# Gated linear attention on one core: a chunk of 64 tokens in place of 128

## The chip, the cores and the metric

The kernel runs on one core of a Trainium2 chip. The core's engines work side by side, each through its own instruction list in order: TensorE (PE in the profile; PEld is its weight load), VectorE (DVE), ScalarE (ACT), GpSimd (POOL), and SyncE (SP), which issues the DMAs. The metric is device time in microseconds (us).

## The reference, cut to what matters

```python
B, H, S, D = 4, 8, 768, 48
mag = np.sqrt(a_re * a_re + a_im * a_im)
scale = np.minimum(mag, 0.999) / (mag + 1e-06)          # a_n = a * scale
for t in range(S):                                       # per batch and head
    S_re, S_im = ar * S_re - ai * S_im + kv, ar * S_im + ai * S_re   # kv = outer(k_t, v_t)
    y[:, :, t] = einsum('bhd,bhde->bhe', q[:, :, t], S_re)
x = y as (B, S, H * D)                                   # 384 channels
xk, xr = mu * x + (1 - mu) * x_prev                      # two mixes, token t with t - 1
out = sigmoid(xr @ w_r) * (maximum(xk @ w_k, 0) ** 2 @ w_v)      # d_ff = 1024
```

A complex state per head is rotated and decayed at each token, and read by q. The result goes through a channel mix with three weight matrices.

## The kernel before, in words

The work is cut into 8 **units** of U = 384 tokens (4 batches, two halves each; `half` is 0 or 1). A unit has three parts.

- `gate(u)`, on ACT and DVE: cumulative log decay and angle over the tokens, by which k and q are multiplied in place in `G[u]` (`kqc` and `kqs` are its cosine and sine rows, channels on partitions). With that, the recurrence is plain causal linear attention over stacked rows of 2 x 48 per head.
- `attend(u)`. `stack(h)` moves a head's rows by DMA into a tile `kq[h]` with k in `[:, 0]` and q in `[:, 1]`. The tokens form NC = 3 chunks of P = 128. `scores(h)` (tile `sc`, one PSUM bank) multiplies k by q within each chunk, and DVE multiplies by a causal mask into `pt`. `advance(c)` transposes the keys of chunk c (`tr`, three per part, copied by ACT into `kt`), multiplies them by the values (`up`, 96 x 384), and DVE adds this to the running `state`. `values(p)`, for a pair of heads, adds values times `pt` (`f0`) and state times q (`f1`) in one bank `y`; the two heads go to partitions 0 to 63 and 64 to 111, the two column halves of the array. ACT copies `y` to `ys`, DMAs carry it to `X[u]`.
- `mix(u)`: `x` split in a high and a low part, `z` (11 blocks of nine matmuls of 128 x 384), squared relu into `hhi` and `hlo`, `o` (8 blocks of nine), the gate and the store. These matmuls are float32r, one load and one matmul each. The attention's products are float32: each appears in the trace as **two** load-and-matmul pairs, whereas the instruction rows shown further down count products.

Before the first units, weights are converted on ACT, DVE and POOL (`wx`).

`Plan` sets the order: every piece of work is an op with an engine, a cost, data it reads and writes, and slots that it uses (PSUM banks `ps` 5, `kq` 6, `pt` 3, `v` 5, `ys` 1 ...). It computes due times backwards, simulates the engines, and emits instructions in the order that this gives; each engine then runs its list as written and waits where data are missing. `attend(u)` is laid beside `mix(u - 1)`, so PE's list mixes the two, and `gate(u + 2)` is laid under them.

Of the kernel before, what the change touches and what calls it, by code (L numbers as in the profile page):

```python
# [30 lines left out]
YS = 3  # L31
# [23 lines left out]
PTS = 3  # L55
# [184 lines left out]
def tile_kernel(ctx, tc, gat, vt, w_all, mu, slow_g, slow_v, out):  # L240
# [40 lines left out]
    def op_dma(n, f, **kw):  # L281
# [6 lines left out]
    mask = keep.tile([P, P], F32, name="mask")  # L288
    nc.gpsimd.memset(mask, 1.0)
    nc.gpsimd.affine_select(out=mask, in_=mask, pattern=[[1, P]], compare_op=ALU.is_ge,  # L290
                            fill=0.0, base=0, channel_multiplier=-1)
# [13 lines left out]
    state = [keep.tile([2 * D, C], F32, name=f"state{i}") for i in range(NC)]  # L305
# [8 lines left out]
    def open_mix(stack):  # L314
# [5 lines left out]
                wx=WBUFS, g=GP, v=5, sq=1, m=1, ph=1, kq=KQ, kt=2, pt=PTS, xt=1, ys=YS)  # L320
# [8 lines left out]
    def mix(u):  # L329
# [51 lines left out]
        def gate_r(mt):  # L381
# [10 lines left out]
            op_pe(1.45, mul, reads=parts(1) + [("w", W_R + ct) for ct in range(NT)], writes=[("z", u, mt)],  # L392
# [7 lines left out]
        def first(j):  # L400
# [23 lines left out]
            op_pe(1.45, mul, reads=parts(0) + [("w", W_K + 2 * j)], writes=[("f", u, j)], uses=[sp, part_slot[0], sr, sh])  # L424
# [5 lines left out]
        def second(j):  # L430
# [8 lines left out]
            op_pe(1.45, mul, reads=[("hhi", u, j), ("hlo", u, j), ("w", W_V + 2 * j)] + [("o", u, j - 1)] * (j > 0),  # L439
# [22 lines left out]
    with ExitStack() as fast:  # L462
# [71 lines left out]
        def gate(u):  # L534
# [17 lines left out]
            def load_v(c):  # L552
                def f():
                    v = ap.tile([P, C], F32, tag="v", name="v", bufs=5)
# [158 lines left out]
        def attend(u):  # L713
# [6 lines left out]
            def stack(h):  # L720
# [3 lines left out]
                def move(r0, n, i):  # L724
                    def f():
                        if h not in kq:
                            kq[h] = ap.tile([2 * D, 2, U], F32, tag="kq", name="kq", bufs=KQ)
                        ct, o = r0 // P, r0 - h * D
                        s = slice(r0 - ct * P, r0 - ct * P + n)
                        nc.sync.dma_start(out=kq[h][i * D + o:i * D + o + n], in_=G[u][s, ct, 2 * i:2 * i + 2])  # L730
# [18 lines left out]
            def advance(c):  # L749

                sk, su = slot("kt"), slot("ps")
                n = half * NC + c

                def turn(part):
                    sp = slot("ps")

                    def f0():
                        t["tr", c, part] = ps.tile([P, 512], F32, tag="ps", name="tr")[:, :C]
                        for ct in range(NT):
                            nc.tensor.transpose(out=t["tr", c, part][:, ct * P:(ct + 1) * P],  # L760
                                                in_=G[u][:, ct, 2 * part, c * P:(c + 1) * P], identity=ident)

                    def f1():
                        if ("kt", c) not in t:
                            t["kt", c] = ap.tile([P, H, 2, D], F32, tag="kt", name="kt")
                        nc.scalar.copy(out=t["kt", c][:, :, part], in_=t["tr", c, part].rearrange("p (h d) -> p h d", d=D))  # L766
                    op_pe(0.34, f0, heat=0.5, reads=[("kqs" if part else "kqc", u, ct) for ct in range(NT)],
# [4 lines left out]
                new, old = state[(n + 1) % NC], state[n % NC]  # L772

                def up():
                    t["up", c] = ps.tile([P, 512], F32, tag="ps", name="up")[:2 * D, :C]
                    for h in range(H):
                        nc.tensor.matmul(t["up", c][:, h * D:(h + 1) * D],  # L777
                                         lhsT=t["kt", c][:, h].rearrange("p a d -> p (a d)"),
                                         rhs=V[u][c][:, h * D:(h + 1) * D], start=True, stop=True)

                def add():
                    if n:
                        nc.vector.tensor_tensor(out=new, in0=t["up", c], in1=old, op=ALU.add)
                    else:
                        nc.vector.tensor_copy(new, t["up", c])
                op_pe(1.28, up, heat=0.5, reads=[("kt", u, c, 0), ("kt", u, c, 1), ("v", u, c)], writes=[("up", u, c)],
                      uses=[su, sk, v_slot[u][c]])
                op_dve(U, add, reads=[("up", u, c)] + [("S", n % NC)] * (n > 0), writes=[("S", (n + 1) % NC)], uses=[su])

            def scores(h):  # L790
                pt_slot[h], sp = slot("pt"), slot("ps")

                def f0():
                    t["sc", h] = sc = ps.tile([P, NC, P], F32, tag="ps", name="sc", padded_shape=[P, 4, P])
                    for c in range(NC):
                        nc.tensor.matmul(sc[:, c], lhsT=kq[h][:, 0, ts(c, P)], rhs=kq[h][:, 1, ts(c, P)], start=True, stop=True)  # L796

                def f1():
                    pts[h] = ap.tile([P, NC, P], F32, tag="pt", name="pt", bufs=PTS)
                    nc.vector.tensor_mul(pts[h], t["sc", h], mask.unsqueeze(1).to_broadcast([P, NC, P]))  # L800
                op_pe(0.65, f0, heat=0.75, reads=t["st", h], writes=[("sc", u, h)], uses=[sp, pt_slot[h], kq_slot[h]])
                op_dve(U, f1, reads=[("sc", u, h)], writes=[("pt", u, h)], uses=[sp, pt_slot[h]])

            def values(p):

                sp, sy = slot("ps"), slot("ys")
                hs = 2 * p, 2 * p + 1
                inter = [c for c in range(NC) if half or c]

                def part(j):  # L810
# [197 lines left out]
```

## Time and profile before

| | |
|---|---|
| runs | 477.48, 477.81, 482.08 us; median 477.81 |
| span of the profiled execution | 476.8 us (first to last instruction; 1.0 us under the median; no other time is given for that execution) |
| PE | 415.8 us busy, 87% of the span, 2898 matmuls |
| PE's weight loads | 383.5 us busy, 80% |
| DVE | 379.5 us busy, 80% |
| ACT | 297.5 us busy, 62% |
| DMA | 59.98 MB, 126 GB/s on average |

A busy time is the sum of an engine's instruction times, overlaps counted once. Matmuls overlap each other, so the cost of a piece on PE is read as the distance from its start to the start of what follows, in the timeline.

### The profile page before, as it was taken

To read this page: it belongs to the slowest core of one execution; us is meant where nothing else is said; L and a number is where in the kernel's file an instruction comes from. 1 tells how busy PE (TensorE), PEld (TensorE's weight loads), DVE (VectorE), ACT (ScalarE), POOL (GpSimd) and SP (SyncE) were. 2 spreads that over 40 slices of the span, in tenths; PEclk is the share of its full clock that TensorE was granted. 3 is DMA by queue.
4 is the path that set the end of the run, shared out by engine and by line. 5 is a ranking of instruction groups with operands and counts; after the bars stand their busy time and mean duration, and the time that the engine had idled before them with its cause. 6 is when DMAs were issued, how large, how long until landed. Compare 5 with 4: busy or idle time off the path is not lost.

```text
span 476.8 us, 7877 instructions
## 1 busy us (share of the span) xinstructions
PE 415.8 (87%) x2898; PEld 383.5 (80%) x2898; DVE 379.5 (80%) x618; ACT 297.5 (62%) x490; POOL 26.6 (6%) x38
## 2 busy tenths in 40 slices
PE   0008896989868999999999999999999999999994
PEld 0007784979767889988999799989997999899994
DVE  0899989969999898978899888978998894339232
ACT  7869625398739769745884788468957552334530
POOL 1003014031300000000000000000000000000000
PEclk9999756699957899999999999999999999999998
DMA  8997066316107255336433643273421252110101
GB/s 286 408 412 149 1 212 205 80 51 235 52 23 181 70 212 142 85 99 236 114 98 91 234 133 91 76 255 101 118 63 62 72 120 86 40 28 1 50 1 56
DMA packets 25918, 59.98 MB, mean 126 GB/s; under 512 B 5392, under 2 KB 14608, under 8 KB 25872
## 3 DMA queue, kind: packets, MB, share of 16 engines
q1 hardware_dynamic: 25872, 59.40, 40.3%
q8 instruction: 25, 0.41, 0.4%
q14 instruction: 21, 0.17, 0.1%
HBM read 31.07 MB, written 4.72 MB: 75 GB/s over the span
## 4 chain that ended last, share of the span: by engine, by line
PE 63%; DVE 17%; issue 7%; ACT 7%; DMA 3%; POOL 1%; SPq 1%; ACTq 0%; POOLq 0%; DVEq 0%
PE z L374 25%; PE o L437 19%; PE sc L796 7%; PE y L819 4%; PE up L777 4%; PE y L827 3%; PE tr L760 2%; DVE pt L800 2%; ACT sq L261 2%; DMA raw<-in_w_all 2%; DVE wx L509 2%; DVE m L630 1%; DVE ph L658 1%; DMA g<-in_gat 1%; ACT L258 1%
## 5 line engine op out<-in xcount | busy, mean ns | idle before, releaser
L374 PE MATMUL z<-x,w 128*128 128x384 f32 x792 | 155.8, 345 | 1.2 <-ACT r L411 1.0
L374 PEld LDWEIGHTS z<-x,w 128*128 128x128 f32 x792 | 137.8, 191 | 5.7 <-issue 1.9
L437 PE MATMUL o<-hhi,w 128*128 128x384 f32 x384 | 103.3, 351 | 0.6 <-DVE hhi L419 0.6
L437 PEld LDWEIGHTS o<-hhi,w 128*128 128x128 f32 x384 | 70.0, 194 | 3.2 <-issue 1.9
L437 PE MATMUL o<-hlo,w 128*128 128x384 f32 x192 | 66.8, 348 | 4.7 <-DVE hlo L423 4.6
L796 PE MATMUL sc<-kq 96*128 96x128 f32 x384 | 60.5, 309 | 2.8 <-ACT r L411 2.4
L796 PEld LDWEIGHTS sc<-kq 96*128 96x128 f32 x384 | 55.0, 217 | 7.2 <-ACT r L411 3.2
L760 PE MATMUL tr<-ident,g 128*128 128x128 f32 x120 | 22.9, 325 | 42.5 <-DVE g L697 42.4
L411 ACT ACTIVATE r<-z 128x384 f32<-128x384 f32 x64 | 30.9, 485 | 45.3 <-PE z L374 45.3
L760 PEld LDWEIGHTS tr<-ident,g 128*128 128x128 f32 x120 | 17.5, 168 | 45.9 <-issue 32.9
L800 DVE TENSOR_TENSOR pt<-sc,mask 128x384 f32<-128x384 f32 x64 | 34.8, 550 | 18.9 <-PE sc L796 18.0
L419 DVE CAST hhi<-h 128x384 fp32r<-128x384 f32 x64 | 22.6, 355 | 31.2 <-ACT h L415 17.8
L697 DVE TENSOR_TENSOR g<-g,r 128x768 f32<-128x768 f32 x48 | 43.0, 951 | 2.9 <-ACT r L261 2.7
L437 PEld LDWEIGHTS o<-hlo,w 128*128 128x128 f32 x192 | 37.3, 194 | 6.4 <-DVE hlo L423 6.4
L261 ACT ACTIVATE sq<-m 128x1152 f32<-128x1152 f32 (+2 forms) x27 | 27.7, 1057 | 21.0 <-DVE m L639 17.5
L777 PEld LDWEIGHTS up<-v,kt 128*96 128x96 f32 x320 | 35.5, 194 | 3.7 <-ACT kt L766 3.7
L777 PE MATMUL up<-v,kt 128*96 128x48 f32 x320 | 36.4, 277 | 1.6 <-ACT kt L766 1.6
L423 DVE TENSOR_TENSOR hlo<-h,hhi 128x384 fp32r<-128x384 f32 x64 | 34.6, 550 | 0.9
L357 ACT CAST x<-xm 128x384 fp32r<-128x384 f32 x48 | 24.1, 512 | 16.4 <-DVE xm L349 15.0
L819 PE MATMUL y<-pt,v 128*48 128x128 f32 (+1 forms) x384 | 32.3, 299 | 1.6 <-DVE pt L800 1.5
L415 ACT ACTIVATE h<-r 128x384 f32<-128x384 f32 x64 | 32.9, 522 | 0.9
L819 PEld LDWEIGHTS y<-pt,v 128*48 128x48 f32 (+1 forms) x384 | 23.1, 139 | 8.8 <-issue 4.8
(73 smaller groups left out, 552.5 us busy)
## 6 DMA issues: line engine op xcount, KB each, us to landing
kq<-g SPq DMA_DIRECT2D x96, 144.0 KB, 3.0
g<-in_gat SPq DMA_DIRECT2D x18, 768.0 KB, 6.0
raw<-in_w_all SPq DMA_DIRECT2D x9, 768.0 KB, 11.5
g<-in_gat SPq DMA_DIRECT2D x12, 384.0 KB, 7.1
v<-in_vt SPq DMA_DIRECT2D x24, 192.0 KB, 2.8
out_t<-y SPq DMA_DIRECT2D x24, 192.0 KB, 2.1
xt<-ys SPq DMA_DIRECT2D x48, 72.0 KB, 2.3
kq<-g SPq DMA_DIRECT2D x32, 96.0 KB, 2.3
```

Of the source, the lines that this page charges most:

```text
L261: nc.scalar.activation(out=out, in_=in_, func=func, **kw)
L374: nc.tensor.matmul(z, lhsT=wt[s[0]][:, part, s[1]], rhs=r[which][:, ct], start=n == 0, stop=n == 3 * NT - 1)
L411: nc.scalar.activation(out=t["r", j], in_=t["f", j], func=AF.Relu)
L415: nc.scalar.activation(out=t["h", j], in_=t["r", j], func=AF.Square)
L423: nc.vector.tensor_tensor(out=t["lo", j], in0=t["h", j], in1=t["hi", j].bitcast(F32), op=ALU.subtract)
L437: nc.tensor.matmul(tiles["o", mt], lhsT=wt[W_V + 2 * j][:, part, ts(mt, P)], rhs=r, start=j == 0 and n == 0, stop=j == NJ - 1 and n == 2)
L697: nc.vector.tensor_tensor(out=g[:, ct, 2 * i:2 * i + 2], in0=g[:, ct, 2:4], in1=t["r"][:, ct, 1 - i:2 - i].to_broadcast([P, 2, U]), op=ALU ...
L760: nc.tensor.transpose(out=t["tr", c, part][:, ct * P:(ct + 1) * P], in_=G[u][:, ct, 2 * part, c * P:(c + 1) * P], identity=ident)
L777: nc.tensor.matmul(t["up", c][:, h * D:(h + 1) * D], lhsT=t["kt", c][:, h].rearrange("p a d -> p (a d)"), rhs=V[u][c][:, h * D:(h + 1) * D ...
L796: nc.tensor.matmul(sc[:, c], lhsT=kq[h][:, 0, ts(c, P)], rhs=kq[h][:, 1, ts(c, P)], start=True, stop=True)
L800: nc.vector.tensor_mul(pts[h], t["sc", h], mask.unsqueeze(1).to_broadcast([P, NC, P]))
L819: nc.tensor.matmul(t["y", p][rows, ts(c, P)], lhsT=V[u][c][:, cols], rhs=pts[hs[j]][:, c], start=c == 0, stop=False)
```

## The change

Attention works by sub-chunks of SB = 64 tokens. Scores are computed within 64 tokens only: for each chunk two products of 64 x 64, one for the first 64 tokens, written to partitions 0 to 63, and one for the others, to partitions 64 to 127 (column halves of the array). `scores(g)` takes two heads at once, since they fit one bank. A state is kept after every 64 tokens (NS = 6 states of 112 rows, cosine rows at 0 to 47, sine rows at 64 to 111, zeros between); `up` is made for both sub-chunks in two banks, from key rows 0 to 63 or 64 to 127 (row half of the array) into partitions 0 to 63 or 64 to 111 (column half), so in quarters of the array. `values(v)` takes four heads: for every sub-chunk the state of its beginning times q (112 rows, column halves), then values times `pt` (quarters), into two banks, one for each sub-chunk. In half 1 the last chunk is now advanced too, by its first 64 tokens, as its second 64 need a state. `kq` tiles are kept tiles with 112 rows; `pt` has 2 buffers, `ys` is one tile for four heads, `v` has 4 buffers. Some costs in the plan differ.

```diff
+KR = HR + D
+SB = P // 2
+NS = 6
-YS = 3
+YS = 1
-PTS = 3
+PTS = 2
...
-            op_pe(1.45, mul, reads=parts(1) + ...
+            op_pe(1.58, mul, reads=parts(1) + ...
...
             def advance(c):
-                sk, su = slot("kt"), slot("ps")
+                sk = slot("kt")
+                subs = (0,) if half and c == NC - 1 else (0, 1)
+                su = [slot("ps") for _ in subs]
+                rows = SB * len(subs)
...
                     for h in range(H):
-                        nc.tensor.matmul(t["up", c][:, h * D:(h + 1) * D],
-                                         lhsT=t["kt", c][:, h].rearrange("p a d -> p (a d)"),
-                                         rhs=V[u][c][:, h * D:(h + 1) * D], start=True, stop=True)
+                        keys = t["kt", c][:, h].rearrange("p a d -> p (a d)")
+                        for i in range(2):
+                            for s in subs:
+                                r = slice(s * SB, s * SB + SB)
+                                nc.tensor.matmul(t["up", c, s][i * HR:(KR if i else HR), h * D:(h + 1) * D],
+                                                 lhsT=keys[r, i * D:(2 * D if i else HR)],
+                                                 rhs=V[u][c][r, h * D:(h + 1) * D], start=True, stop=True)
...
-            def scores(h):
+            def scores(g):
...
-                    for c in range(NC):
-                        nc.tensor.matmul(sc[:, c], lhsT=kq[h][:, 0, ts(c, P)], rhs=kq[h][:, 1, ts(c, P)], start=True, stop=True)
+                    for i, h in enumerate(hs):
+                        for c in range(NC):
+                            for s in range(2):
+                                q = slice(c * P + s * SB, c * P + s * SB + SB)
+                                nc.tensor.matmul(sc[s * SB:s * SB + SB, i, c], lhsT=kq[h][:, 0, q], rhs=kq[h][:, 1, q],
+                                                 start=True, stop=True)
...
-            def values(p):
+            def values(v):
...
+                    for n in inter:
+                        c, s = n // 2 % NC, n % 2
+                        for h in hs:
+                            add(h, c, s, state[n % NS], kq[h][:, 1, c * P + s * SB:c * P + s * SB + SB], False)
                     for c in range(NC):
+                        for h in hs:
+                            for s in range(2):
+                                r = slice(s * SB, s * SB + SB)
+                                add(h, c, s, V[u][c][r], pts[h // 2][r, h % 2, c], c == NC - 1 and h // 2 == gs[1])
```

Two places in the instruction lists show what this moves. The first is on PE, in the attention of the fourth unit (a second half, `state_87` to `state_89` being its three states). Before, the values of a pair of heads and its state products stand apart, with a state update and a mix block between them here.

```order
L819 MATMUL y<-pt,v 64x128
L819 MATMUL y<-pt,v 48x128
L777 MATMUL up<-v,kt 96x48 x8
L374 MATMUL z<-x,w 128x384 x9
L827 MATMUL y<-kq,state_87 64x128
L827 MATMUL y<-kq,state_87 48x128
L827 MATMUL y<-kq,state_88 64x128
```

In the changed kernel, at the same place, PE has the state products of four heads for six states (`state_88` to `state_93`; `kq_94` to `kq_97` are the four heads) in one run, and right behind their last, shown here, the values.

```order
L849 MATMUL y<-kq_94,state_93 64x64
L849 MATMUL y<-kq_95,state_93 48x64
L849 MATMUL y<-kq_96,state_93 64x64
L849 MATMUL y<-kq_97,state_93 48x64
L849 MATMUL y<-pt,v 64x64 x2
L849 MATMUL y<-pt,v 48x64 x2
```

So there are two such runs in a unit, where there were eight pieces, and each changes from column halves to quarters in its middle. Counted along PE's list, the places where neighbours use the array differently (full width, column halves, quarters) are 118 before and 131 after.

The second place is on DVE, in the states of a first half (the seventh unit's): of three instructions for the unit, the second and the third.

```order
L783 TENSOR_TENSOR state_89<-up,state_88 96x384
L360 TENSOR_TENSOR x<-xm,x 128x384
L620 TENSOR_SCALAR m<-m 128x1152
L746 MEMSET xt 128x3
L783 TENSOR_TENSOR state_87<-up,state_89 96x384
```

Now there are six for such a unit, the first five of them here, between the mix's `x` and `xm` and two mask products (`pt`, each of two heads now).

```order
L802 COPY state_89<-up 112x384
L367 TENSOR_TENSOR x<-xm,x 128x384 x2
L800 TENSOR_TENSOR state_90<-up,state_89 112x384
L356 SCALAR_TENSOR_TENSOR xm<-dx,mu_sb,xt 128x384
L800 TENSOR_TENSOR state_91<-up,state_90 112x384
L823 TENSOR_TENSOR pt<-sc,mask 128x384
L367 TENSOR_TENSOR x<-xm,x 128x384
L800 TENSOR_TENSOR state_92<-up,state_91 112x384
L823 TENSOR_TENSOR pt<-sc,mask 128x384
L800 TENSOR_TENSOR state_93<-up,state_92 112x384
```

So each state is a step in a chain of five or six additions, where it was one of two or three.

Over the whole list DVE has 32 `pt` instructions for 64, and 44 on states for 20; all have 384 elements a row. ACT copies `kt` 48 times for 40. The DMAs of `kq` and `ys` stay 160 and 80 in number.

More of the change, by code (lines that the diff above doesn't have):

```diff
@@ L304, in tile_kernel @@
     nc.gpsimd.memset(tiny, 2.0 ** -60)
-    state = [keep.tile([2 * D, C], F32, name=f"state{i}") for i in range(NC)]
+    state = [keep.tile([KR, C], F32, name=f"state{i}") for i in range(NS)]
+    stacked = [keep.tile([KR, 2, U], F32, name=f"kq{i}") for i in range(KQ)]
+    for x in stacked:
+        nc.gpsimd.memset(x[32:HR], 0.0)
     last = keep.tile([P, NT, 1], F32, name="last")
@@ L391, in out_ @@
                 nc.scalar.copy(out=zr[u][:, mt], in_=tiles["z", mt])
-            op_pe(1.45, mul, reads=parts(1) + [("w", W_R + ct) for ct in range(NT)], writes=[("z", u, mt)],
+            op_pe(1.58, mul, reads=parts(1) + [("w", W_R + ct) for ct in range(NT)], writes=[("z", u, mt)],
                   uses=[sp, part_slot[1]])
@@ L438, in mul @@
                                          start=j == 0 and n == 0, stop=j == NJ - 1 and n == 2)
[L439 removed]
+            op_pe(1.58, mul, reads=[("hhi", u, j), ("hlo", u, j), ("w", W_V + 2 * j)] + [("o", u, j - 1)] * (j > 0),
                   writes=[("o", u, j)], uses=[so, *hs[j]])
@@ L765, in f1 @@
                             t["kt", c] = ap.tile([P, H, 2, D], F32, tag="kt", name="kt")
-                        nc.scalar.copy(out=t["kt", c][:, :, part], in_=t["tr", c, part].rearrange("p (h d) -> p h d", d=D))
-                    op_pe(0.34, f0, heat=0.5, reads=[("kqs" if part else "kqc", u, ct) for ct in range(NT)],
+                        nc.scalar.copy(out=t["kt", c][:rows, :, part], in_=t["tr", c, part].rearrange("p (h d) -> p h d", d=D))
+                    op_pe(0.35, f0, heat=0.5, reads=[("kqs" if part else "kqc", u, ct) for ct in range(NT)],
                           writes=[("tr", u, c, part)], uses=[sp, sk, g_slot[u]])
@@ L781, in add @@
[L781 to L788, printed above, removed]
@@ new lines, in advance, with add @@
+                op_pe(0.95, up, heat=0.5, reads=[("kt", u, c, 0), ("kt", u, c, 1), ("v", u, c)],
+                      writes=[("up", u, c, s) for s in subs], uses=[*su, sk, v_slot[u][c]])
+                for s in subs:
+                    n = 2 * (half * NC + c) + s
+                    def add(n=n, s=s):
+                        new, old = state[(n + 1) % NS], state[n % NS]
+                        if n:
+                            nc.vector.tensor_tensor(out=new, in0=t["up", c, s], in1=old, op=ALU.add)
+                        else:
+                            nc.vector.tensor_copy(new, t["up", c, s])
+                    op_dve(U, add, reads=[("up", u, c, s)] + [("S", n % NS)] * (n > 0), writes=[("S", (n + 1) % NS)],
+                           uses=[su[s]])
```

128 lines of the change are left out of this document (70 added, 58 removed).

## The prediction

> **What bounds the kernel now.** The page's first section says which engines are full, its slices say when, and its chain says which of them the end waits for.
>
> ```profile
> PE 415.8 (87%) x2898; PEld 383.5 (80%) x2898; DVE 379.5 (80%) x618; ACT 297.5 (62%) x490; POOL 26.6 (6%) x38
> PE   0008896989868999999999999999999999999994
> DVE  0899989969999898978899888978998894339232
> PEclk9999756699957899999999999999999999999998
> PE 63%; DVE 17%; issue 7%; ACT 7%; DMA 3%; POOL 1%; SPq 1%; ACTq 0%; POOLq 0%; DVEq 0%
> PE z L374 25%; PE o L437 19%; PE sc L796 7%; PE y L819 4%; PE up L777 4%; PE y L827 3%; PE tr L760 2%; DVE pt L800 2%; ACT sq L261 2%; DMA raw<-in_w_all 2%; DVE wx L509 2%; DVE m L630 1%; DVE ph L658 1%; DMA g<-in_gat 1%; ACT L258 1%
> ```
>
> A slice is 11.9 us. From the thirteenth on PE is full; before that it has holes and a clock as low as 0.5. The chain gives the attention's lines (`sc`, `y`, `up`, `tr`) 20% of the span and the mix 44%. I then asked for the busy times by stage: the start, two stretches of two units each, and the end.
>
> ```profile
> core 0: us, PE busy (x) PEld busy (x) DVE busy (x) ACT busy (x) POOL busy (x), PEclk, DMA share, GB/s
> 24.00:146.00 122.00, 94.72 (x562) 83.07 (x562) 115.03 (x161) 76.49 (x115) 23.80 (x11) 0.82 0.47 143
> 205.90:302.70 96.80, 95.69 (x725) 89.11 (x725) 84.86 (x139) 68.33 (x114) 0.19 (x1) 1.00 0.45 135
> 302.70:399.40 96.70, 95.59 (x725) 89.07 (x725) 84.18 (x143) 61.51 (x105) 0.19 (x1) 1.00 0.39 113
> 399.40:476.80 77.40, 71.03 (x465) 67.30 (x463) 29.77 (x64) 25.98 (x54) 0.75 (x10) 0.98 0.10 33
> ```
>
> The start is DVE's: 115.03 of 122 us, 94%. The two units' stretches are PE's, 95.69 of 96.80 at full clock, with DVE at 88%. So a microsecond saved on PE counts from the third unit on, as far as DVE lets it, and little in the first two.
>
> **What a step costs on PE.** Matmuls overlap, so I read start to start in the timeline. Three excerpts at full clock:
>
> ```profile
> 106.71 0.87 PE L819 MATMUL y<-pt,v 128*64 128x128 f32 x12
> 107.41 0.83 PE L827 MATMUL y<-kq,state 96*48 96x128 f32 x12
> 108.17 0.62 PE L437 MATMUL o<-hhi,w 128*128 128x384 f32 x2
> ...
> 207.45 0.87 PE L827 MATMUL y<-kq,state 96*64 96x128 f32 x12
> 208.25 1.84 PE L374 MATMUL z<-x,w 128*128 128x384 f32 x9
> 209.93 1.50 PE L796 MATMUL sc<-kq 96*128 96x128 f32 x12
> 211.18 1.80 PE L374 MATMUL z<-x,w 128*128 128x384 f32 x9
> 212.92 0.87 PE L819 MATMUL y<-pt,v 128*64 128x128 f32 x12
> ...
> 237.16 1.72 PE L374 MATMUL z<-x,w 128*128 128x384 f32 x9
> 238.72 0.51 PE L437 MATMUL o<-hhi,w 128*128 128x384 f32 x2
> ```
>
> Twelve score matmuls take 211.18 - 209.93 = 1.25 us, 0.104 each. Twelve of `y`, alternating between column halves, take 0.80 alone (207.45 to 208.25), and two such pieces together 1.46 (106.71 to 108.17). So twelve more cost 0.66, 0.055 each, and 0.14 is the piece's own entry and exit. The halves therefore run at the same time: each takes 0.110 for 128 moving columns, hence 0.055 for 64. A `z` before a `y` takes 1.74 (211.18 to 212.92), among its like 1.56, so 0.18 more. A change between full and halved array costs 0.07 (half of 0.14) to 0.16 (half of 0.32); I take 0.12.
>
> ```profile
> 249.92 1.47 PE L760 MATMUL tr<-ident,g 128*128 128x128 f32 x12
> 251.32 0.87 PE L819 MATMUL y<-pt,v 128*64 128x128 f32 x12
> 252.12 2.92 PE L777 MATMUL up<-v,kt 128*96 128x48 f32 x32
> 254.97 0.65 PE L827 MATMUL y<-kq,state 96*64 96x128 f32 x8
> ```
>
> Transposes take 1.40 / 12 = 0.117 for 128 weight columns, `up` 2.85 / 32 = 0.089 for 96, though it moves only 48: both are 0.92 ns a weight column, so weight loads bound them. A load of 64 columns is then 0.058, just over its 0.055 of moving columns, and **0.058 us is my step**: one load and one matmul of 64 columns in one part of the array.
>
> Do loads in two halves run side by side too? The first 0.1 us of a `y` piece shows it:
>
> ```profile
> 203.53 0.19 PEld L819 LDWEIGHTS y<-pt,v 128*64 128x64 f32 x4 [0.17 <-issue]
> 203.53 0.32 PE L819 MATMUL y<-pt,v 128*64 128x128 f32 x2
> ```
>
> By 203.60 four loads and two matmuls had begun. One after the other, three loads of 48 to 64 columns need 0.14 us ahead of the fourth. The Trainium skill ("TensorE: Matmul & The Clock Gate", Part 3) says that a weight load overlaps a running matmul only where its row group differs; both halves use all rows, so by it a halved step would cost load plus matmul, 0.113, and scores would gain nothing. The 0.055 per matmul of `y` speaks against that here.
>
> **The change, part by part**, at full clock, all units. The counts of before:
>
> ```profile
> L796 PE MATMUL sc<-kq 96*128 96x128 f32 x384 | 60.5, 309 | 2.8 <-ACT r L411 2.4 <-ACT zr L261 0.4
> L777 PE MATMUL up<-v,kt 128*96 128x48 f32 x320 | 36.4, 277 | 1.6 <-ACT kt L766 1.6
> L819 PE MATMUL y<-pt,v 128*64 128x128 f32 x192 | 31.2, 300 | 0.5 <-DVE pt L800 0.5
> L819 PE MATMUL y<-pt,v 128*48 128x128 f32 x192 | 30.0, 297 | 1.1 <-DVE pt L800 1.0
> L827 PE MATMUL y<-kq,state 96*64 96x128 f32 x160 | 25.6, 293 | 0.0
> L827 PE MATMUL y<-kq,state 96*48 96x128 f32 x160 | 25.2, 290 | 0.0
> ```
>
> - Scores: 384 x 0.104 = 40.0. After, 768 matmuls in two halves, 384 steps x 0.058 = 22.3. **-17.7.**
> - State times q: 320 x 0.055 = 17.6. After, 44 states x 8 heads x 2 = 704, in halves, 352 x 0.058 = 20.4. **+2.8.** Finer sub-chunks move the same columns; the surplus is the state that a first half's first chunk now needs.
> - Values times `pt`: 384 x 0.055 = 21.1. After, 768 of 64 rows and 64 columns. If the four quarters run at once, 192 x 0.058 = 11.1. **-10.0.**
> - `up`: 320 x 0.089 = 28.5. After, 20 full chunks of 64 matmuls in quarters (16 steps) and 4 half chunks of 32 in two quarters (16 steps): 384 x 0.058 = 22.3. **-6.2.**
> - 24 more transposes, of 64 columns: 0.058 to 0.117 each; they still move 128, so I take 0.117. **+2.8.**
> - 13 more changes of mode (131 for 118): 13 x 0.12. **+1.6.**
>
> Sum -26.7. No row shows a product with 64 rows, so the quarters are the unknown. Their lower bound is above; the upper one is row halves that take turns: 0.029 per matmul, values 22.3 (+1.2) and `up` 20 x 32 x 0.058 + 64 x 0.058 = 40.8 (+12.3), and the sum is +3.0.
>
> Six of eight units are PE's: 6/8 x 26.7 = **20.0 us**.
>
> In the first two units PE's clock is low and DVE is late:
>
> ```profile
> 54.51 2.93 PE L796 MATMUL sc<-kq 96*128 96x128 f32 x12
> ```
>
> ```profile
> L800 DVE TENSOR_TENSOR pt<-sc,mask 128x384 f32<-128x384 f32 x64 | 34.8, 550 | 18.9 <-PE sc L796 18.0
> L783 DVE TENSOR_TENSOR state<-up,state 96x384 f32<-96x384 f32 x16 | 8.8, 550 | 3.7 <-PE up L777 3.7
> ```
>
> DVE there has 16 - 8 = 8 `pt` less and 11 - 5 = 6 state instructions more, 0.55 each: -1.1. Its 7.0 us of idle time (122 - 115.03) bound the rest, as part of it waits for scores that take double (2.93 for twelve). I take **3 us** of the 0 to 8.
>
> Later PE's speed meets DVE: a two-unit stretch has 84.86 - 1.1 = 83.8 of DVE in 96.8 - 6.7 = 90.1, 93%, just under the 94% that the start sustains. Each state is now a step in a chain of additions, and DVE's list is strict: what stands behind a state that waits for `up` (`x`, `xm`, `hhi`) waits too, and PE for those. I give back **2.5 us** of 0 to 5 (half of the 13.4 of two stretches is rival 1's case). ACT's 8 more copies of `kt` and the fewer `pt` and `v` buffers I cost at nothing: ACT is busy 68.33 of 96.80 us, and mix blocks of 1.56 us stand between most of these pieces on PE's list. The `ys` DMAs go out in groups of four and six, not two and four, and `ys` has one buffer:
>
> ```profile
> xt<-ys SPq DMA_DIRECT2D x48, 72.0 KB, 2.3
> ```
>
> The mix that reads them comes a unit later, behind the other mix's blocks; where there is none, in the first unit, a landing of 2.3 us more is the price, and it lies in the 0 to 8 above. At the end (399.40 on) the last unit's mix is bare and stays as it is.
>
> Total: 476.8 - 20.0 - 3 + 2.5 = 456.3 span; the median is 1.0 over the span, so **457 us**.
>
> **The rivals.**
>
> 1. *Waits take half of it.* If DVE gets no fuller than its 88% of now, a two-unit stretch needs 83.8 / 0.877 = 95.6 us, and 5.5 of 6.7 are lost in both; with the 2.5 already given back, 457 + 11 - 2.5 = 466. For it: DVE idles for PE in places (18.0 us before `pt`), which is order, not load. Against: 94% in the start. 10%.
> 2. *Quarters are worth no more than halves.* Row halves take turns, the sum is +3.0, x 6/8 = +2.3, and 477.8 + 2 = 480, no change that tells. For it: no row shows row halves at once. Against: column halves share everything but the columns, and do run at once. 14%. The Trainium skill bears on it twice: "TensorEngine Tiling (Array Packing)" (Key Properties) says that such parts work independently, but "TensorE: Matmul & The Clock Gate" (Part 1) puts matmul starts never under about 25 ns apart, which quarters at 0.0145 would break. By that floor, as an estimate, values would cost 19.2 and `up` 35.7, and the time would be about 474; no row here has starts so dense for long.
> 3. *Slower: PE takes products in order.* A float32 product is two pairs on the same part of the array, and the second waits for the first. Should PE not reach past it to the next product, only the ends overlap: two steps for each product, less one shared, 0.062 per product, 0.031 per matmul, whatever the part. All 3648 matmuls (768 + 704 + 768 + 1408) cost 113.1 for 107.2 before; with 2.8 and 1.6 that is +10.3, x 6/8 = +7.7, so **485**. It decides from (107.2 - 4.4) / 3648 = 0.028. Against: two matmuls within 0.07 us at 203.53, when the first needs 0.110. For it: PE must take 3648 pairs where it took 1408, and the densest lasting rate shown is one in 0.055; at that bound they would cost 200.6, and the time be 551. 12%.
>
> **How the numbers follow.** Forecast 64%, rivals 10, 14 and 12. With the lower bounds (steps of 0.055, transposes of 0.058, 7 us at the start, nothing given back) the forecast reaches 446; with a start that gains nothing and 5 given back, 463. The range 446 to 480 holds the forecast, rival 1 and most of rival 2, and leaves rival 3 out. Within 1% (4.8 us, about what a measurement of this kernel can tell from no change) falls rival 2: faster 0.73, same 0.14, slower 0.13.
>
> **What would show it.** In the changed profile: a two-head `sc` piece at about 0.70 + 0.12 us, not 1.25; 64 `up` matmuls in 0.95 to 1.1, not 1.9; a four-head `values` of a second half in 1.4 + 0.7 us plus entry; a two-unit stretch of 89 to 93 us, PE still over 97% busy and DVE near 93%. Wrong would be: `up` or the values at 0.03 per matmul (rivals 2 and 3; scores tell these apart), PE idle behind `hhi` or the states (rival 1), or a granted clock under 1.00 in the two-unit stretches.

## The result, and the profile after

| | before | after |
|---|---|---|
| median of all runs | 479.05 us (20 runs) | 476.43 us (20 runs) |
| ratio after / before | | 0.9943, 95% interval 0.9925 to 0.9962 |
| span of the profiled execution | 476.8 us | 474.4 us |

The change makes the kernel faster by 0.6%, some 2.6 us, where 21 were forecast. The page of the changed kernel: busy times, three rows of slices (11.9 us each), and the chain.

```profile
PE 382.8 (81%) x5162; PEld 351.0 (74%) x5162; DVE 374.5 (79%) x610; ACT 299.9 (63%) x498; POOL 32.3 (7%) x45
PE   0008445879966999979989999999799988999994
DVE  0798999969989889898989799569967898248222
PEclk9999755789978999999999999999899989999998
PE 42%; DVE 28%; ACT 13%; DMA 7%; issue 5%; SPq 3%; POOL 1%; DVEq 0%; ACTq 0%
PE z L381 19%; PE o L444 12%; PE y L849 5%; DVE ph L665 4%; DMA kq<-g 3%; PE sc L818 3%; DVE g L654 3%; DMA g<-in_gat 3%; SPq L736 3%; PE up L789 2%; ACT sq L264 2%; DVE m L637 2%; DVE g L704 2%; DVE xm L356 2%; ACT L261 2%
```

PE has 33 us less to do (415.8 before), and the kernel does not get them. The chain, which was PE for 63%, is now PE for 42%, and the lines that came in or grew are the gate's (`ph`, `m`, `g`, `sq`). DVE's row, which before had nothing under 7 from the tenth slice to the last units, has a 5 and a 6 at 296 to 320 us and a 6 and a 7 at 344 to 368. By stage, the last row being the four units from the first `z` of the third unit to that of the seventh:

```profile
24.00:146.00 122.00, 77.66 (x1118) 67.12 (x1118) 114.35 (x164) 76.58 (x119) 24.70 (x11) 0.82 0.46 141
205.90:302.70 96.80, 91.54 (x1286) 85.70 (x1285) 83.89 (x144) 69.26 (x116) 0.24 (x1) 1.00 0.47 142
302.70:399.40 96.70, 87.79 (x1231) 79.55 (x1230) 81.13 (x133) 63.88 (x107) 0.26 (x1) 0.96 0.36 103
201.90:398.60 196.70, 181.93 (x2528) 167.18 (x2525) 168.19 (x280) 134.46 (x225) 0.50 (x2) 0.98 0.41 120
```

The same four units before:

```profile
205.70:399.20 193.50, 191.29 (x1451) 178.18 (x1449) 169.04 (x282) 130.01 (x219) 0.37 (x2) 1.00 0.42 124
```

So the span splits into a start, four units in the middle, and an end. Three units' attention lies in the start (that of a unit runs beside the mix of the one before), four in the middle and one in the end; the forecast is split likewise, 3.3 us (26.7 / 8) for each unit behind the first two, and 3 for those.

| us | start | four units | end | PE idle in the four units |
|---|---|---|---|---|
| before | 205.7 | 193.5 | 77.6 | 2.2 |
| after | 201.9 | 196.7 | 75.8 | 14.8 |
| after - before, forecast | -6.3 | -13.4, less 2.5 given back | -3.3 | |
| after - before, measured | -3.8 | +3.2 | -1.8 | +12.6 |

In the middle PE's own work fell by 9.4 us (191.29 to 181.93), and its idle time rose by 12.6 (193.50 - 191.29 = 2.2, 196.70 - 181.93 = 14.8). The longest of the waits that make it up, in the stretch 202 to 398 us (total, times, longest):

```profile
PE tr L768 <- DVE g L704: 2.7, 3, 1.7
PE y L849 <- ACT zr L398: 2.4, 1, 2.4
PE o L444 <- DVE hlo L430: 1.8, 2, 1.1
PE sc L818 <- DVE state L802: 1.5, 2, 0.9
PE o L444 <- DVE hhi L426: 1.1, 3, 0.6
PE sc L818 <- DMA kq<-g: 0.8, 1, 0.8
PE sc L818 <- ACT ys L871: 0.7, 1, 0.7
```

No one wait stands out; they are many, each on another piece. The list names what came last at each stop, and nothing in it says why the gate's lines are on the chain.

The pieces on PE, start to start in the timeline, came out as forecast:

```profile
196.56 1.13 PE L789 MATMUL up<-v,kt 64*64 64x48 f32 x64
197.63 0.41 PE L768 MATMUL tr<-ident,g 128*64 128x128 f32 x2
...
220.25 0.92 PE L818 MATMUL sc<-kq 112*64 112x64 f32 x24
221.10 1.83 PE L381 MATMUL z<-x,w 128*128 128x384 f32 x9
222.86 1.61 PE L849 MATMUL y<-kq,state 112*64 112x64 f32 x48
224.41 0.92 PE L849 MATMUL y<-pt,v 64*64 64x64 f32 x48
225.25 1.83 PE L381 MATMUL z<-x,w 128*128 128x384 f32 x9
```

24 score matmuls in 0.85 us (forecast 0.82), 64 of `up` in 1.07 (0.95 to 1.1), 48 state products in 1.55 and 48 values in 0.84.

### The profile page after: what moved, and what is told of

Same layout as the page of the kernel before. It is cut to its first block, busy times and chain, and to the rows that moved or that the text cites. A ratio compares the mean times of both kernels' runs of the same rounds, so it can differ in the third digit from the quotient of the medians.

```text
span 474.4 us, 12425 instructions
## 1 busy us (share of the span) xinstructions
PE 382.8 (81%) x5162; PEld 351.0 (74%) x5162; DVE 374.5 (79%) x610; ACT 299.9 (63%) x498; POOL 32.3 (7%) x45
## 4 chain that ended last, share of the span: by engine, by line
PE 42%; DVE 28%; ACT 13%; DMA 7%; issue 5%; SPq 3%; POOL 1%; DVEq 0%; ACTq 0%
PE z L381 19%; PE o L444 12%; PE y L849 5%; DVE ph L665 4%; DMA kq<-g 3%; PE sc L818 3%; DVE g L654 3%; DMA g<-in_gat 3%; SPq L736 3%; PE up L789 2%; ACT sq L264 2%; DVE m L637 2%; DVE g L704 2%; DVE xm L356 2%; ACT L261 2%
## 5 line engine op out<-in xcount | busy, mean ns | idle before, releaser
L381 PEld LDWEIGHTS z<-x,w 128*128 128x128 f32 x792 | 140.3, 193 | 8.4 <-DVE state L800 2.2
L768 PE MATMUL tr<-ident,g 128*128 128x128 f32 (+1 forms) x144 | 27.7, 311 | 49.3 <-DVE g L704 47.8
L768 PEld LDWEIGHTS tr<-ident,g 128*128 128x128 f32 (+1 forms) x144 | 17.8, 148 | 55.9 <-issue 31.9
L818 PE MATMUL sc<-kq 112*64 112x64 f32 x768 | 31.7, 233 | 8.9 <-DMA kq<-g 2.7
L818 PEld LDWEIGHTS sc<-kq 112*64 112x64 f32 x768 | 26.9, 144 | 15.5 <-issue 6.2
L364 ACT CAST x<-xm 128x384 fp32r<-128x384 f32 x48 | 24.2, 511 | 17.1 <-DVE xm L356 13.6
L789 PEld LDWEIGHTS up<-v,kt 64*48 64x48 f32 (+1 forms) x1408 | 27.0, 139 | 6.8 <-ACT kt L774 3.9
L849 PE MATMUL y<-kq,state 112*48 112x64 f32 (+1 forms) x704 | 25.7, 229 | 7.5 <-DVE state L800 5.1
L849 PEld LDWEIGHTS y<-kq,state 112*48 112x48 f32 (+1 forms) x704 | 23.2, 136 | 11.4 <-DVE state L800 5.3
L789 PE MATMUL up<-v,kt 64*48 64x48 f32 (+1 forms) x1408 | 29.4, 231 | 2.4 <-DVE state L800 1.3
L529 POOL TENSOR_TENSOR w<-wx,w 128x768 fp32r<-128x768 f32 (+1 forms) x10 | 24.5, 2454 | 85.6 <-ACT w L526 85.6
```

What stands on the lines that cost most here:

```text
L381: nc.tensor.matmul(z, lhsT=wt[s[0]][:, part, s[1]], rhs=r[which][:, ct], start=n == 0, stop=n == 3 * NT - 1)
L529: nc.gpsimd.tensor_tensor(out=t["w"][:, :, 1], in0=t["x"], in1=t["w"][:, :, 0].bitcast(F32), op=ALU.subtract)
L789: nc.tensor.matmul(t["up", c, s][i * HR:(KR if i else HR), h * D:(h + 1) * D], lhsT=keys[r, i * D:(2 * D if i else HR)], rhs=V[u][c][r, h ...
L818: nc.tensor.matmul(sc[s * SB:s * SB + SB, i, c], lhsT=kq[h][:, 0, q], rhs=kq[h][:, 1, q], start=True, stop=True)
L849: nc.tensor.matmul(t["y", v][s][rows, h // 2 % 2, c], lhsT=lhsT[:, cols], rhs=rhs, start=(s, h % 2) not in begun, stop=stop)
```

## The experiments

Each is compared with the kernel before, run beside it on the same chip (its medians there: 478.87 to 480.51 us). The expectations call the theories by letters. **P**: PE set the time before, and new waits keep the gain after. **G**: the gate's work on DVE and ACT sets the length of a unit in both kernels. **W**: the PSUM banks do, since `up` and `values` now hold two each. **O**: the order that the plan writes is a matter of chance within some us, or of the changed costs in the plan. **K**, which came up only after the first eight runs: a small copy of the gate stands too late in DVE's list.

**Less work on PE.** Two of the nine `z` matmuls of each block are left out, by the same edit in both kernels; nothing moves in the lists.

```diff
-                    nc.tensor.matmul(z, lhsT=..., rhs=r[which][:, ct], ...)
+                    if part == 0 or ct == 0:
+                        nc.tensor.matmul(z, lhsT=..., rhs=r[which][:, ct], ...)
```

> The kernel before with two of the nine matmuls of each z block left out (176 matmuls, 30 us of PE at 0.173 us each; the low-part weights of two channel blocks are left out of the sums), same order. Theory G (the gate's chain of DVE and ACT instructions sets the length of a unit in both kernels, PE only kept pace before): 474 to 478 us, hardly faster, as with the change. Theory P (PE sets the time of the kernel before, as my prediction had it, and the changed kernel lost its gain in new waits of its own): 455 to 460.

> The changed kernel with the same two of nine z matmuls left out. Theory G: 472 to 476, no gain, since PE already waits. Theory P (waits of the new order on PE's own list): about 455, since the work between the waits is shorter.

Measured: before 461.53 us, ratio 0.9631 (0.9574 to 0.9688); after 460.84, 0.9614 (0.9568 to 0.9659). That is 19.0 us of 30 (the kernel before took 480.51 beside it), and 15.6 of 30 (476.43). So PE's work counted before, and it counts now; the 3.4 us between the two gains lie within the intervals. The four units of the changed kernel then read

```profile
198.80:389.70 190.90, 169.15 (x2438) 151.56 (x2436) 167.55 (x280) 133.99 (x225) 0.50 (x2) 0.98 0.42 123
```

PE idles 21.75 of 190.90 us and they are still only 5.8 us shorter than with all the work: of the 12.8 us less that PE is busy there (181.93 to 169.15), 7.0 turn into waiting.

**Less work in the gate.** Five kinds of DVE instructions of the gate (two clamps of `m`, the running sum of `ph`, two on `r`), 6.4 us in a unit, are left out, the order kept.

```diff
-                    op_dve(2 * U, lambda ct=ct: scan(ct), reads=..., writes=..., uses=[s_ph])
+                    op_dve(2 * U, lambda ct=ct: None, reads=..., writes=..., uses=[s_ph])
...
```

> The changed kernel with five kinds of DVE instruction left out of the gate (the two clamps of m, the running sum of the angle, the clamp of r and its absolute value; 6.4 us a unit, all on the chain from load to rotated keys), order unchanged. Theory G: each of some six units gets up to 6.4 us shorter until PE is full, 440 to 452. Theory P: 472 to 477, as PE's list does not wait for the gate itself.

> The kernel before with the same DVE instructions left out of the gate. Theory G with PE as a second bound just below: 466 to 477, as PE has 1.1 us to give in 96.8. If DVE alone set the time in both kernels: 440 to 452, like the changed one. Theory P: 474 to 478.

Measured: after 458.65 us, ratio 0.9546 (0.9499 to 0.9593), between the ranges of G and of P. Before 466.92, with no interval, as its four runs lie far apart (461.63 to 469.14). By stage both lose 13 us in the start (205.7 to 192.7 before, 201.9 to 188.9 after), which DVE sets. In the four units the changed kernel gains 5.0 (191.7), the kernel before 0.9. In the changed kernel's two-unit stretch DVE is now at 75%, and PE still waits:

```profile
205.90:302.70 96.80, 93.78 (x1339) 88.13 (x1337) 72.45 (x126) 68.29 (x120) 0.39 (x1) 1.00 0.47 140
```

PE idles 12.7 us in the four units here, against 14.8. So it is not the amount of DVE's work: in the four units DVE was busy 146.4 us in place of 168.2, and that took 2 us from PE's idle time. Theory G falls for the four units.

**More banks.** The second and third block of `o` are summed into one bank, and the pool of the others has 6 banks in place of 5, in the tiles alone: the plan and its order stay.

```diff
-    ps = ctx.enter_context(pool("ps", 5, space=PSUM))
+    ps = ctx.enter_context(pool("ps", 6, space=PSUM))
...
-                        tiles["o", mt] = pso.tile([P, 512], F32, tag=f"o{mt}", name="o")[:, :U]
+                        tiles["o", mt] = tiles["o", 1] if mt == 2 else pso.tile([P, 512], F32, tag=f"o{mt}", name="o")[:, :U]
```

> The changed kernel with six PSUM banks for the ps tiles instead of five, same instruction order (the third bank of o is given up: the second and third block of o are summed in one bank, same matmuls, so two of three output blocks are not the reference's). Theory W (PE now waits for banks, which values and up take two at a time and which DVE and ACT free late; in the middle, from z of the third unit to z of the seventh, 7.8 of its 14.8 us of idle time end on a copy or addition that frees a bank): the middle gets 5 to 8 us shorter, 468 to 472. Theory G (the gate's chain): nothing, 474 to 477. Theory O (the order itself, made with other costs): nothing, 474 to 477.

> The same sixth bank for the kernel before, same order. PE has 2.2 us of idle time in its middle: 477 to 480 by every theory; a gain of 5 us or more would say that banks bound the kernel before too and that this says nothing of the change.

Measured: after 472.96 us, 0.9875 (0.9828 to 0.9922), 3.5 less than without; before 478.16, 0.9968 (0.9944 to 0.9992). The banks are a small part. PE's waits moved on to the next thing (`hlo`, 3.3 us in the four units in place of 1.8).

**Another order.** The plan's cost of a mix block set back from 1.58 to 1.45, and the changed buffer counts put into the kernel before.

```diff
-            op_pe(1.58, mul, ...)
+            op_pe(1.45, mul, ...)
```

```diff
-YS = 3
+YS = 1
-PTS = 3
+PTS = 2
...
-                wx=WBUFS, g=GP, v=5, ...
+                wx=WBUFS, g=GP, v=4, ...
```

> The changed kernel with the plan's cost of a mix block put back from 1.58 to 1.45, which undoes one part of the change and gives another order. Theory O: the order loses the gain; then this moves by 5 us or more, downwards to 465 to 470 if 1.58 is the wrong number. Theories W and G: 473 to 479, the same waits in other places.

> The kernel before with the buffers of the change: v 4 for 5, pt 2 for 3, ys 1 for 3 (pt and ys of one and two heads, so tighter than in the change). If fewer buffers take the gain back: 485 to 495. If not: 477 to 482.

Measured: 481.03 us, 1.0024 (0.9996 to 1.0052), and 472.97, 0.9843 (0.9794 to 0.9891). Neither the cost nor the buffers are to blame. But an edit that leaves every piece of work as it is moves the time by 5 to 7 us, and the order is all that can have gained the 7, since fewer buffers by themselves can only add waits: a forecast of this kernel is no finer than that, and a gain by one order is no proof of a cause. These two stay unexplained in their details.

**The late copy.** The gate keeps the angle's running sum in one buffer, `ph`. `keep_phi` is a DVE copy of nine columns, 0.16 us, out of it into `stat`. In DVE's timeline of the kernel before it stands between the buffer's two other late readers (gate 5; units and gates counted from 0):

```profile
273.37 0.16 DVE L667 COPY stat<-ph 128x9 f32<-128x9 f32 x1
273.49 1.36 DVE L678 SCALAR_TENSOR_TENSOR r<-r,ph 128x1152 f32<-128x1152 int32 x1
```

In the changed kernel:

```profile
273.24 1.35 DVE L685 SCALAR_TENSOR_TENSOR r<-r,ph 128x1152 f32<-128x1152 int32 x1
...
296.22 0.16 DVE L674 COPY stat<-ph 128x9 f32<-128x9 f32 x1
```

It runs 21.6 us after the last other reader. Until then the buffer is held, and the plan does not let the next gate begin, whose first instructions on ACT are these:

```profile
295.34 1.17 ACT L591 ACTIVATE m<-g 128x1152 f32<-128x1152 f32 x1
296.42 1.26 ACT L595 ACTIVATE ph<-g,re_min 128x1152 f32<-128x1152 f32 x1
```

The `m` there does not use the buffer, but its place in ACT's list comes from the plan; `ph` starts as the copy ends. At gate 6 the same: last reader to 328.2, copy at 350.2, next gate from 347.4, and here ACT's row names the copy as what it waited for:

```profile
350.42 1.26 ACT L595 ACTIVATE ph<-g,re_min 128x1152 f32<-128x1152 f32 x1 [1.88 <-DVE stat L674]
```

In the kernel before these gates begin at 273.4 and 323.8. The runs of the changed kernel with less PE work, with less gate work and with six banks all have the copy 21 to 22 us late in these two gates as well. The cause is in the plan's rules. A copy whose result is read late, or (second halves) by nothing, gets a late due time, and DVE takes the ready piece that is due first; that the copy holds a buffer for which others wait does not count. In the old order the copy got its turn between the two readers; in the new one DVE does other pieces for 22 us first. Four slices of 25 us show what follows, in the changed kernel:

```profile
300.00:325.00 25.00, 25.00 (x363) 23.53 (x363) 17.23 (x26) 18.91 (x34) 0.00 (x0) 1.00 0.45 156
325.00:350.00 25.00, 21.50 (x326) 19.16 (x325) 23.40 (x40) 12.90 (x21) 0.00 (x0) 0.93 0.35 85
350.00:375.00 25.00, 24.30 (x329) 23.14 (x328) 17.16 (x31) 20.60 (x34) 0.26 (x1) 1.00 0.30 89
375.00:400.00 25.00, 20.29 (x237) 17.02 (x237) 24.83 (x41) 13.99 (x24) 0.00 (x0) 0.93 0.29 71
```

Where the late gate is still on ACT, DVE runs short (17.23 and 17.16 of 25 us, the third figure); when its DVE work comes, all at once, DVE is full (23.40, 24.83) and the mix's and the attention's DVE pieces come late, so that PE has 21.50 and 20.29 us, and a granted clock of 0.93. PE's waits in these two slices are for the late gate's own products (`g`, 2.7 us) and for the mix's `hlo` and `hhi` (2.6 us). The remedy is one line: the first of the other readers (`f0`) is made to depend on the copy, which so gets its due time.

```diff
-                op_dve(n, f0, rate=2, reads=kk("ph", c), writes=kk("r1", c), uses=[s_ph, s_r])
+                op_dve(n, f0, rate=2, reads=kk("ph", c) + kk("phi", c), writes=kk("r1", c), uses=[s_ph, s_r])
```

> The changed kernel with one dependency added in the plan: the scaling of the angle (f0 in b0) comes after keep_phi, the 0.16 us DVE copy of the angle's ends into stat, so that the plan no longer puts that copy off. In the changed kernel it runs 21.6 and 22.0 us after the last other reader of ph in the sixth and seventh gate (in the kernel before 1.5 us ahead of its end), it holds the one ph buffer, and the next gate begins 0.9 us before and 2.8 us before at the earliest it can. Theory K (that copy holds up the gates, the gates hold up PE): the middle shrinks from 196.6 to 184 to 190, the total to 460 to 467. Theory O (list orders differ by some 5 us by chance, this does nothing of its own): 472 to 481. Theory W (banks): 473 to 477.

> The same dependency in the kernel before, where the copy is late in the second gate alone (31 us) and PE is full in the middle. Theory K: the middle stays near 190 to 194, the start may gain a little, 472 to 480. If it gains as much as the changed kernel, the copy has nothing to do with where the change's gain went.

> The same dependency in the changed kernel with the plan's mix cost put back to 1.45 (481.0 without it; there the copy is late in the third and eighth gate). Theory K: 460 to 470, so the gain does not hang on one order. Theory O: anything from 472 to 481.

Measured: after **462.39 us, 0.9647 (0.9611 to 0.9683)**, 14 us less than the changed kernel and faster than both; before 479.69, 1.0008 (0.9984 to 1.0032); after with the old cost 469.11, 0.9799 (0.976 to 0.9839), 12 less than with that cost alone. That last gain is no proof of the same cause: with the old cost alone the copies of gates 5 and 6 are not late; those of gates 1 and 2 are, by 23 and 19 us. By stage it gains 5.6 us in the start, 5.4 in the four units and 2.0 in the end. The slices again, now of the changed kernel with the early copy:

```profile
300.00:325.00 25.00, 25.00 (x364) 23.53 (x363) 21.16 (x33) 15.72 (x28) 0.00 (x0) 1.00 0.50 160
325.00:350.00 25.00, 23.94 (x394) 21.84 (x396) 22.52 (x41) 21.14 (x35) 0.00 (x0) 1.00 0.39 105
350.00:375.00 25.00, 25.00 (x299) 23.91 (x293) 22.68 (x37) 17.05 (x29) 1.07 (x1) 1.00 0.33 86
375.00:400.00 25.00, 24.00 (x421) 22.22 (x421) 16.19 (x35) 11.39 (x26) 0.00 (x0) 1.00 0.39 104
```

DVE's work is more even (no slice of it is full), PE is at 97.9 of 100 us, and the clock at 1.00. Its whole page: PE 380.2 us, DVE 376.6, as much work as in the changed kernel. The four units:

```profile
199.60:387.10 187.50, 179.17 (x2584) 166.68 (x2581) 169.88 (x286) 134.79 (x228) 1.26 (x2) 1.00 0.43 127
```

**The lateness by itself.** As an order alone is worth 5 to 7 us, the copy was then moved on purpose. In the changed kernel: early in gates 5 and 6 alone; early in all but these; early in all but gate 6. In the kernel before: late in gates 5 and 6, by two amounts, with all of PE's work and with 30 us less. The edit that makes it late, with `f` of the unit that runs beside the gate, or `z` of the one after:

```diff
-                op_dve(10, keep_phi, reads=kk("ph", c), writes=kk("phi", c), uses=[s_ph])
+                if u in (5, 6):
+                    held_copy.append(lambda: op_dve(10, keep_phi, reads=kk("ph", c) + [("f", u - 2, 6)], ...))
+                else: ...
...
             run(mix(u), t + a, t + e)
+            run([held_copy.pop() for _ in held_copy[:]], 0, 0)
```

The later ones have `("z", u - 1, 0)` for `("f", u - 2, 6)`, and `after_early_56` only `kk("phi", c) * (u in (5, 6))` among `f0`'s reads.

> The kernel before, with the small copy out of the angle buffer (keep_phi) of gates 5 and 6 made to wait for block f 6 of the mix that runs beside that gate, so that DVE reaches it some 15 to 25 us after the last other reader of the buffer, as in the changed kernel. Nothing is left out. Theory K (the late copy costs because the next gate cannot begin, whatever the chunk): the next gates begin and end about as late as in the changed kernel (gate 7 ends near 393 us, not 382), but here PE's work fills more of each unit, so that a part of the lateness is covered: 3 to 10 us slower, 482 to 490 us. If the lateness costs nothing where PE bounds the units: 478 to 481 us, and the copy matters only once PE is faster. Theory O (the order's chance alone): anything from -7 to +5 us, with gate 7's end unchanged by the copy's place.

> The reverse: the changed kernel, in which only the copies of gates 5 and 6 are put early; those of the other gates stand where the plan puts them. Nothing is left out. Theory K, with the cost in the two gates whose copy was some 22 us late: 464 to 469 us, most of the 14 us of after_early_phi. If the cost came from gate 1 or gate 7 (also late in the changed kernel), or theory O: 473 to 479 us.

> The changed kernel with the copy out of the angle buffer early in all gates (as in after_early_phi, 462.4 us), except in gates 5 and 6, where it is made to wait for block f 6 of the mix that runs beside that gate: 42 instructions of DVE behind the place where the buffer's last other readers stand in gate 5, as in the changed kernel, and 9 in gate 6. Nothing is left out. Theory K (the held buffer starves DVE, and then PE waits for the late gate): most of the gain goes again, 468 to 476 us, with a 25 us stretch behind gate 5 in which DVE is under 75% busy. Theory O (the early-copy kernels had luckier orders): 459 to 466 us.

> The kernel before with two of the nine z matmuls of each block left out, as in before_less_pe (461.5 us), and with the copies of gates 5 and 6 late as in before_late_phi. Theory K with cover (the lateness costs nothing only as long as PE's own work is the longer): with 30 us less of PE work the cover is gone, 467 to 475 us, with PE idle in the last two units. If the lateness costs the chunk of 64 alone: 459 to 464 us.

> The changed kernel with early copies in all gates except gate 6, whose copy waits for block z 0 of the unit after: 40 instructions of DVE behind the last other reader's place (34 in the changed kernel). Nothing is left out. Theory K, narrowed (the lateness costs what of it reaches gate 7's end): gate 7 ends at 388 us or later and the time is 468 to 476 us. If only the chance of an order made the changed kernel slow: 460 to 466 us.

> before_less_pe (461.5 us; two of the nine z matmuls of each block left out) with the copies of gates 5 and 6 later still, both held until block z 0 of the unit after: 41 instructions of DVE behind their places (42 and 34 in the changed kernel). Theory K with cover: TensorE has as little work here as in the changed kernel, so the lateness costs 5 to 14 us, 466 to 476 us, with PE idle in the fifth and sixth unit. If the lateness costs only with the chunk of 64: 459 to 463 us.

> The kernel before, all of its work, with the copies of gates 5 and 6 as late as in before_less_pe_later_phi. Theory K with cover: PE has 30 us more to do than there, so a part of the lateness is hidden: 480 to 486 us, and the loss is smaller than there. Without cover the loss would be the same as there, 5 to 14 us.

Measured, with the kernels they are to be held against. "Late by" is the time from the end of the buffer's last other reader to the copy, in gates 5 and 6 (negative: the copy comes first); gate 7's end shows what of it is passed on, as each gate begins only when the buffer is free.

| kernel | late by, us | gate 7 ends | us | ratio, interval |
|---|---|---|---|---|
| changed, early in all | -3.0, -3.4 | 375.9 | 462.39 | 0.9647 (0.9611 to 0.9683) |
| changed, early in 5, 6 alone | -3.0, -3.5 | 379.5 | 464.75 | 0.9680 (0.9628 to 0.9732) |
| changed, late in 5 (6 a little) | 24.3, 3.6 | 378.7 | 464.51 | 0.9679 (0.9628 to 0.9730) |
| changed, late in 6 | -3.0, 24.2 | 384.9 | 472.97 | 0.9862 (0.9817 to 0.9906) |
| changed | 21.6, 22.0 | 392.7 | 476.43 | 0.9943 (0.9925 to 0.9962) |
| before | -1.5, -1.5 | 382.4 | 479.05 | |
| before, late | 15.3, 17.9 | 391.3 | 479.60 | 0.9993 (0.9971 to 1.0015) |
| before, later | 28.3, 21.6 | 403.8 | 488.29 | 1.0171 (1.0119 to 1.0223) |
| before, less PE | -1.5, -1.5 | 374.3 | 461.53 | 0.9631 (0.9574 to 0.9688) |
| before, less PE, late | 13.9, 16.8 | 383.2 | 461.29 | 0.9595 (0.9534 to 0.9656) |
| before, less PE, later | 26.1, 22.0 | 392.4 | 471.62 | 0.9826 (0.9776 to 0.9876) |

The kernel before with the later copy, DVE's timeline and two of the 25 us slices:

```profile
275.21 1.36 DVE L682 SCALAR_TENSOR_TENSOR r<-r,ph 128x1152 f32<-128x1152 int32 x1
...
304.87 0.16 DVE L667 COPY stat<-ph 128x9 f32<-128x9 f32 x1
```

```profile
300.00:325.00 25.00, 25.00 (x222) 22.39 (x220) 13.52 (x23) 16.48 (x28) 0.00 (x0) 1.00 0.47 158
325.00:350.00 25.00, 22.05 (x131) 19.83 (x128) 20.48 (x32) 15.21 (x22) 0.00 (x0) 1.00 0.24 66
```

- The early copy in two gates brings 11.7 of the 14 us, and the lists are the same up to gate 5. So that is where the loss of the changed kernel lies.
- Late in gate 6 alone costs 10.6 us (472.97 for 462.39). Late in gate 5 alone costs 2.1, less than I expected of both gates: one unit becomes longer, and the next ones make it up, since gate 7 is hardly later (378.7 for 375.9). Each of these edits also changes the order behind it, and 2.1 us is less than an order alone can do; the others are more.
- In the kernel before, copies 15 to 18 us late cost nothing, which I had not expected, and copies 22 to 28 us late cost 9.4 us (488.29 for 478.87 beside it) and leave the same hole in DVE's work (13.52 of 25 us), followed by PE's (22.05).
- My reading after the first of these, that PE's own work hides the lateness, fell: with 30 us less of PE's work the later copies cost 10.1 us (471.62 for 461.53), with all of it 9.4. Slack in the gate may be what hides it: the gate is ready early enough to be some 17 us late for nothing, and at 22 us it is not. That is not shown, and gate 7's end alone does not bear it out: 9 us later cost nothing in the kernel before (391.3 for 382.4), and 10.6 in the changed kernel (384.9 for 375.9, late in gate 6). Where the cost begins, and whether the chunk of 64 makes it begin earlier, was not measured.
- Nor does a hole in DVE's work always cost. The kernel before with the copies 15 to 18 us late has one as deep as the changed kernel's (16.83 us, then 24.72), and PE stays at 25.00 and 24.54:

```profile
350.00:375.00 25.00, 25.00 (x197) 22.18 (x196) 16.83 (x26) 18.34 (x31) 0.00 (x0) 1.00 0.19 50
375.00:400.00 25.00, 24.54 (x183) 23.52 (x183) 24.72 (x43) 13.64 (x25) 1.58 (x1) 1.00 0.33 85
```

So theory K holds for the loss of the changed kernel: ACT waits for the copy, and moving it by 22 to 24 us in gate 6, alone or with gate 5, costs or brings 9.4 to 14 us in both kernels, where an order alone (O) was worth 5 to 7. The cost does not need the chunk of 64: the kernel before pays it too, when its copies are 22 to 28 us late. Whether the same lateness costs more with the chunk of 64 stays open.

## Why the prediction was wrong

1. **PE's steps** were right. Scores 0.85 us for a piece (0.82 forecast), `up` 1.07 for 64 (0.95 to 1.1), values 0.84 / 48 = 0.0175 per matmul (0.0145 and the piece's exit). With the clock at 1.00 (early copy), PE's busy time in the four units fell by 191.29 - 179.17 = 12.1 us; the sum of steps said 13.4. One reading of the prediction is off by one, and nothing hangs on it: the thirteenth slice has PE at 8 tenths, and it is full from the fourteenth on.
2. **Rivals 2 and 3** fell with it: row halves in turn would be 0.029 per matmul, products in order 0.031, and `up` ran at 1.07 / 64 = 0.0167. The loss is in none of the products.
3. **The step that failed** is "I give back 2.5 us of 0 to 5". In the four units PE's idle time rose by 12.6 us, and its busy time fell by 9.4 only. The same 288 matmuls of `o` there keep PE busy for 86.0 us, and for 82.5 with the early copy. The granted clock was 0.96 in the second stretch, where 1.00 was forecast; how much of this is the clock, and how much matmuls that stand alone after a wait, was not taken apart. Against the -10.9 forecast the four units came out at +3.2. Of these 14.1 us, 9.2 went with the early copy (196.70 to 187.50). In the whole span the copy is 474.4 - 460.6 = 13.8 us of the 18.1 by which 456.3 was missed.
4. **The reason for the give-back** was half right. I named states and DVE's strict list, and took DVE's load (93%) for the measure. The list did it, but by an order in which a copy of 0.16 us kept a buffer for 22 us. DVE was no fuller than 87% in the first two-unit stretch (83.89 of 96.80). Rival 1 (466 us, DVE no fuller than 88%) had the direction and about half of the size, and its signs came true (87%, PE idle behind `hlo`, `hhi` and the states, a clock under 1.00). But 88% is no bound of DVE: with the early copy it did get to 91% there (87.88 of 96.80).
5. **What was costed at nothing** was the order of the gate. I read the diff's effect on PE's list and on the states; I did not follow the one-buffer tiles of the gate (`ph`, `m`, `sq`) through the new list. The place of `keep_phi` could be read from the lists before any run: in the changed kernel it stands 42 instructions of DVE behind its buffer's other readers.
6. **Start and end.** The start gave 3.8 us of the 6.3 and, with all copies early, 6.1. With those of gates 5 and 6 alone, which come after the start, it gave 4.7: so 0.9 is what the same list gives from one execution to the next, and 1.4 may be the copy of gate 1, which in the changed kernel runs at 94.0 us, 24 after its buffer's other readers; in the kernel before, that copy moved from 31 us late to early gained nothing (479.69 for 479.83). The end gave 1.8 of 3.3, with the early copy 4.1. In the changed kernel 24 score and 32 `up` matmuls, some 1.4 us by the rows above, fall into the end, where in the kernel before and with the early copy they fall into the four units: at equal work its four units would be 1.4 us worse than the table shows, and its end 1.4 better.
7. **What is left.** With the early copy the change is worth 462.39 for 479.69 us, 17.3 of 21. The rest lies in the four units, -6.0 where -10.9 was forecast: PE idles 8.3 us there (187.50 - 179.17) against 2.2. That was not taken apart further. Nor is it known why the plan with the old mix cost is 5 to 7 us slower, with the late copy and without, though its copies in gates 5 and 6 are not late.

## What to carry to other kernels

When a change takes work off the engine that bounds a kernel whose order a plan writes, look in the new lists, for each tile with a single buffer, at the distance from its last reader but one to its last: a tiny reader that nobody needs soon can hold the buffer and with it everything that comes next. Here the profile showed it as a hole in an engine that is not the bound, followed by a stretch in which that engine is full and the bounding one waits, in pieces too small to stand out in the list of waits; one such hole cost nothing, so the hole alone is no proof. Before a gain from one reordered version is believed, move the suspected instruction both ways, also in the other kernel: here a mere reordering was worth up to 7 us.

## What the runs showed of the hardware

Products in quarters of the array start much more densely than I could show before: 64 matmuls of 64 rows in 1.07 us, 0.0167 apart, and 48 in 0.84. The Trainium skill ("TensorE: Matmul & The Clock Gate", Part 1) says that matmuls never start less than about 25 ns apart; these rows, of matmuls that take turns among the four quarters, do not agree, and the measurement decides. The Trainium skill (the same page, Part 3) has weight loads overlap running matmuls only where the row group differs; the scores, in column halves that use the same rows, took 0.85 / 24 = 0.035 us for a load and a matmul of 64 columns each, where a load and its matmul one after the other would be 0.113 by the prediction's estimates from its rows (0.058 and 0.055), and half of that, 0.057, even with both halves side by side; so here, too, the trace speaks against it.
